# Top-128 rows of a gated scan through one expert: a last gather with a single wait, halved steps in the last expert block, another last search, one transfer for the weights

## Chip, cores and metric

One core of a Trainium2 chip runs the whole program. The metric is device time in microseconds (us). Times inside the program are counted from the start of the profiled span.

## The reference

Two steps, in float32. First a gated linear scan over 6208 positions, for 4 batches and 256 channels:

```python
f = lower_bound + (1 - lower_bound) * sigmoid(f_logit);  i = 1 - f
for t in range(S):                        # S = 6208
    h = f[:, t] * h + i[:, t] * x[:, t]
    y[:, t] = h
```

Then, for each batch, the 128 positions with the highest score go through one expert, and only these rows change:

```python
scores = einsum('bsd,d->bs', y, w_gate)
top = argpartition(-scores[b], 128)[:128]
xe = y[b, top]                            # 128 x 256
ye = maximum(xe @ w1, 0) @ w2             # w1 256 x 1024, w2 1024 x 256
out[b, top] = xe + sigmoid(scores[b, top])[:, None] * ye
```

## The kernel before

**Stream.** Channels lie on the 128 partitions in two halves (`h`), positions run along the free axis. The 6208 positions of a batch are cut into units of up to four blocks of 256. For each unit SP loads gate logits (`ft`) and inputs (`xt`), ACT makes the gates, POOL and DVE weigh the inputs, DVE runs the scan (L291), PE computes scores into the PSUM tile `score` (L300, one half of it for each batch in turn) and transposes the result into `pt`, ACT or DVE copies it to `ym`, and SP stores `ym` to the batch's output tensor (L327).

**Search** (`choose`, L372). For each batch: ACT copies the scores out (`keep`), PE spreads them over 32 lanes (`lanes`), DVE finds 16 candidates a lane and their places (`top`, `where`), PE broadcasts the candidates (`row`), DVE counts for four groups of candidates how many are greater (`ranks`), POOL and DVE make one-hot marks of the ranks (`marks`), PE pulls the indices out (`pull`), and DVE writes them to `idx` (`finish`, L458). A flag (`tell`, `flag`) says whether a lane had too many; its sum over the batches decides about the rare slow path below.

**Expert** (`stages`, L493, `experts`, L561). POOL gathers the 128 rows from the stored output by an indirect DMA (`fetch`, L502); it must wait for all stores of that batch and for `idx`. PE transposes the rows (`turn_in`, L508), ACT copies them out (`take`, L515), DVE computes the gate's score (`ask`, L524) and ACT its sigmoid (`opened`, L528). PE multiplies by w1 (`up`, L536: 8 groups x 2 halves, in float32 two records each), ACT applies relu to 4 groups at a time (L544), PE multiplies by w2 (`down`, L549: 8 groups), DVE adds the result to the rows (`mix`, L552) and POOL scatters them back (`scatter`, L556).

**Slow path** (`redo_all`, L636). DVE sums the flags into `total` (L638). POOL, PE, ACT and DVE each load `total` into a register (L639) and jump over the code of the slow path (L640), which is not run when the sum is zero. On POOL that code is some 7,000 instructions long. Each engine reads its instructions in order, so what stands behind the jump on an engine waits for the jump. The last batch's `mix` and `scatter` stand behind it.

**Order.** A planner (`Plan`, L58) simulates queues with a cost and a due time for each step and emits the steps in the order of their simulated start, so the order on each engine is fixed when the program is built. Waiting is by semaphores. On POOL an instruction with several waits is preceded by sequencer instructions (EVENT_SEMAPHORE) that carry two waits each.

Of the kernel before, what the change touches and what calls it, by code (L numbers as in the profile page):

```python
# [9 lines left out]
F32 = mybir.dt.float32  # L10
BF16 = mybir.dt.bfloat16
I32 = mybir.dt.int32
# [20 lines left out]
RUSH = [3]  # L33
XFER = 2.48
AHEAD, BACKLOG, STORE = 30.0, 4.0, 180.0
TURN, PUT, FIND, EXPERT = 20.0, 5.0, [0.0, -100.0, -50.0, -100.0], [240.0, -100.0, 80.0, 200.0]
WEIGHTS_AT = [6, 7]
AFTER = "pull"
HOP, PE_HOP, ISSUE, DONE = 0.14, 0.22, 1.75, 0.75
# [139 lines left out]
def gated_scan_moe(tc, xin, fin, lbwg, w1, w2, outs, cap):  # L179
    nc = tc.nc  # L180
    v, a, pe, g = nc.vector, nc.scalar, nc.tensor, nc.gpsimd
    with ExitStack() as ctx:
# [41 lines left out]
        w1t = const.tile([P, NH, F], F32, name="w1t")  # L224
        w2t = const.tile([P, NF, D], F32, name="w2t")
# [24 lines left out]
        def unit(i):  # L250
# [83 lines left out]
            plan.tile(("ym", i), (small, "y"), [("store", i)])  # L334
# [35 lines left out]
            add("sp", XFER * k, store, p + STORE, [*puts, ("store", i - 1)], ("store", i), late=DONE)  # L370

        def choose(b):  # L372
# [17 lines left out]

            def lanes():
                for k in range(BLK // LANE):
                    q0, c = (0, k - 6) if k >= 6 else (1, k + 2)
                    pe.matmul(acc[:LANE, c : c + 8 * (NBLK - q0) + 1 : 8], wide[b][:, k * LANE : (k + 1) * LANE],
                              order[:, q0 : NBLK + 1], start=True, stop=True)

            def top(k):
                if k == 0:
                    st["ci"] = new("ci", [LANE, 2, LEVELS])
                    st["at"] = new("at", [LANE, LEVELS], U32)  # L400
                    st["rest"] = new("rest", [LANE, NPOS])
                here, ci = acc[:LANE, :NPOS], st["ci"]
                if k == 0:
                    v.max(out=ci[:, 0, :TOP], in_=here)
                if k == 1:
                    v.max_index(out=st["at"][:, :TOP], in_max=ci[:, 0, :TOP], in_values=here)
                if k == 2:
                    v.match_replace(out=st["rest"], in_to_replace=ci[:, 0, :TOP], in_values=here, imm_value=LOW)
                if k == 3:
                    v.max(out=ci[:, 0, TOP:], in_=st["rest"])  # L410

            def spread():
                st["diag"] = d = new("dg", [LANE, RANKED, LANE])
                eye = acc[:LANE, A_ID : A_ID + LANE] if b in RUSH else ident[:LANE, :LANE]
                (v if b in RUSH else g).tensor_tensor(d, eye.unsqueeze(1).to_broadcast([LANE, RANKED, LANE]),
                                st["ci"][:, 0, :RANKED].unsqueeze(2).to_broadcast([LANE, RANKED, LANE]), ALU.mult)
# [4 lines left out]
            def number_of():  # L421
                (v if b in RUSH else g).tensor_copy(st["ci"][:, 1], st["at"])

# [3 lines left out]
            def own(what):  # L427
                for q in range(4):
                    pe.matmul(acc[q * LANE : (q + 1) * LANE, A_OWN + what * OWN : A_OWN + (what + 1) * OWN], ident[:LANE, :LANE],
                              st["ci"][:, what].rearrange("p (a q) -> p a q", q=4)[:, :, q], start=True, stop=True)  # L430

            def mine():
                st["mine"] = new("mine", [P, OWN])
                v.tensor_copy(st["mine"], acc[:, A_OWN : A_OWN + OWN])

            def ranks(k):
                if k == 0:
                    st["rank"] = new("rank", [P, OWN])
                junk = new("junk", [P, ROW], BF16)
                v.tensor_scalar(junk, acc[:, :ROW], st["mine"][:, k : k + 1], None, ALU.is_gt, ALU.add,  # L440
                                accum_out=st["rank"][:, k : k + 1])

            def number():
                v.tensor_scalar(vals[:, :, 0], acc[:, A_OWN + OWN : A_OWN + 2 * OWN], float(LANE), None, ALU.mult)

            def marks(k):
                if k == 0:
                    st["hot"] = new("hot", [P, OWN, P], BF16)
                (v if b in RUSH and k == OWN - 1 else g).tensor_scalar(st["hot"][:, k], slot, st["rank"][:, k : k + 1], None, ALU.is_equal)  # L449

# [20 lines left out]
            chain("pe", 0.8, lanes, extra=[("flag", b - 1), ("wgrow",), *[("mix", c) for c in range(b) if c not in APART]])  # L471
            for k in range(4):
                chain("dve", 0.4, lambda k=k: top(k))
            rush = b in RUSH
# [3 lines left out]
            m = chain("dve", 0.16, mine)  # L478
            w = chain("dve" if rush else "pool", 0.17, number_of, after=chain("dve", 0.44, where, after=t), extra=[d])
            r = chain("pe", 0.75, row, after=d)  # L480
            n = chain("dve", 0.17, number, after=chain("pe", 0.15, lambda: own(1), after=w, extra=[r]))
            marked = [n]
            for k in range(OWN):
                r = chain("dve", 0.74, lambda k=k: ranks(k), after=r, extra=[m])
                here = rush and k == OWN - 1
                marked.append(chain("dve" if here else "pool", 0.25 if here else 0.62, lambda k=k: marks(k), after=r))
            last[0] = r
# [5 lines left out]
        def stages(b, st):  # L493
            def fetch():
                again = "found" in st
                spot = st.get("spot")
                st["xe"] = spot[:, 3 * BLK : 4 * BLK] if again else rows[b % 2]
                st["res"] = spot[:, BLK : 2 * BLK] if again else moe.tile([P, D], F32, name="res", bufs=2)
                if again:
                    g.memset(st["xe"], 0.0)  # L500
                st["from"] = bass.IndirectOffsetOnAxis(ap=(st["found"] if again else chosen[b])[:cap, :], axis=0)
                g.indirect_dma_start(out=st["xe"][:cap, :], out_offset=None, in_=outs[b][:, :], in_offset=st["from"],  # L502
                                     bounds_check=S - 1, oob_is_err=False)

            def turn_in():
                st["px"] = st["bank"][1] if "found" in st else hold(("pm", b, 0), [P, TP * P], "pm")
                for h in range(NH):
                    pe.transpose(st["px"][:, h * P : (h + 1) * P], st["xe"][:, h * P : (h + 1) * P], ident)  # L508

# [16 lines left out]
            def opened():  # L526
                st["open"] = moe.tile([P, 1], F32, name="open" + "2" * ("found" in st), bufs=2)
                a.activation(st["open"], st["gate"], ACTF.Sigmoid)  # L528

# [20 lines left out]

            def mix():
                v.scalar_tensor_tensor(st["res"], st["py"][:, :D], st["open"], st["xe"], ALU.mult, ALU.add)  # L552
# [5 lines left out]

            return fetch, turn_in, take, ask, opened, up, relu, down, mix, scatter

        def experts(b):  # L561
            fetch, turn_in, take, ask, opened, up, relu, down, mix, scatter = stages(b, {})
# [4 lines left out]
            add("pool", 1.04, fetch, p0, [("st", b), ("store", last_unit[b])], k("fetch"))  # L567
            add("sw", 0.36, None, p0 - 1e3, [k("fetch")], k("xe"), late=LAND[b])
            add("pe", 0.36, turn_in, p0, [k("xe"), ("moe", b - 1, "down", NF - 1)], k("flip"), takes=[("pm", b, 0)])
            plan.tile(("pm", b, 0), ("pt", "pt"), [("xT", b)])  # L570
            add("act", 0.38, take, p0 - 1, [k("flip")], ("xT", b))
# [5 lines left out]
            for f in range(NF):  # L577
                add("pe", 0.49, lambda f=f: up(f), p0, [("xT", b), k("up", f - 1)], k("up", f), takes=[("pm", b, 1 + f // TP)] if f % TP == 0 else [])
# [3 lines left out]
            for f in range(NF):  # L582
# [71 lines left out]
        def weights(t, src, k):  # L654
            nc.sync.dma_start(t, src.rearrange("(p k d) -> p k d", p=P, k=k))
# [3 lines left out]
        for k, (t, src, n) in enumerate([(w1t, w1, NH), (w2t, w2, NF)]):  # L659
            add("sp", XFER, lambda t=t, src=src, n=n: weights(t, src, n), 20.0 * WEIGHTS_AT[k], [("x", WEIGHTS_AT[k])], ("w", k), late=DONE)  # L660
# [6 lines left out]
        plan.tile(("warm",), ("gt", "gt"), [("moe", B - 1, "down", 0)])  # L667
        add("pe", FILL, lambda: fill(True), 20.0 * N, [("forget", N - 1, 1)], ("warm",), takes=[("warm",)])
        plan.warm, plan.fill = (("warm",), ("moe", B - 1, "down", 0)), fill
# [45 lines left out]
```

## Time and profile before

| what | us |
|---|---|
| median of 3 runs (lowest, highest) | 212.48 (211.96, 212.50) |
| profiled execution, its own time | 211.78 |
| its span from first to last instruction | 209.8 |
| what lies around the span | 1.98 |

| engine | busy us | share of the span |
|---|---|---|
| PE (TensorE matmul) | 160.9 | 77% |
| DVE (VectorE) | 158.2 | 75% |
| ACT (ScalarE) | 154.1 | 73% |
| POOL (GpSimd) | 160.1 | 76% |
| DMA queue of SP (share of 16 engines' span) | | 89.6% |

How to read it: no engine is busy all the time, and the share of the SP queue's transfers is an average over a long stream in which the DMA engines are full and a tail of some 20 us in which they are nearly idle. The two have to be looked at apart. Rows with a name such as POOLq or PEldq are those of an engine's sequencer: waits, register loads, jumps.

### The profile page before, as it was taken

Reading aid. Unit: us, or ns where it says so; the run is one execution under the profiler, and the core shown is the slowest. Engines: PE = TensorE matmul, PEld = TensorE weight load, DVE = VectorE, ACT = ScalarE, POOL = GpSimd, SP = SyncE. Lnnn points to the kernel's source line nnn. Section 1 sums busy time; section 2 is a strip of 40 time slices with the busy share of each in tenths; the row PEclk is TensorE's granted clock in tenths of the full one; section 3 lists DMA queues with packets and bytes.
Section 4 is the critical chain, followed back from the end, with each engine's and each line's share of the span. In section 5 each row is a group of like instructions: output and inputs, shape, how many; then the busy total and the mean of one; then the engine's idle time right before and its main releaser. Section 6 shows DMA issues by size and latency. Waiting matters only on the chain. (4 is left out here: it accounts for less than half of the span.)

```text
span 209.8 us, 3352 instructions
## 1 busy us (share of the span) xinstructions
PE 160.9 (77%) x1174; PEld 104.5 (50%) x1174; DVE 158.2 (75%) x200; ACT 154.1 (73%) x206; POOL 160.1 (76%) x154
## 2 busy tenths in 40 slices
PE   0686749677878776773878998778789998989880
PEld 0233435444344444441435886444388856559670
DVE  1488599988799998868598969899795899472100
ACT  4698989989869899799769959768978787312110
POOL 4389999875989999987999895797999899223101
PEclk9997976999555899997559999995559999999996
DMA  6999999999999999999999999999999999992100
GB/s 203 407 428 426 426 425 419 429 428 420 414 433 426 422 422 427 426 428 425 419 428 428 418 420 430 423 417 425 430 426 425 419 422 417 430 417 82 52 5 28
DMA packets 13684, 79.69 MB, mean 380 GB/s; under 512 B 1760, under 2 KB 2016, under 8 KB 5728
## 3 DMA queue, kind: packets, MB, share of 16 engines
q1 hardware_dynamic: 13136, 78.39, 89.6%
q0 software_dynamic: 384, 1.05, 1.3%
q8 instruction: 11, 0.18, 0.3%
q14 instruction: 9, 0.07, 0.1%
q10 hardware_dynamic: 144, 0.00, 0.0%
HBM read 53.48 MB, written 25.95 MB: 379 GB/s over the span
## 5 line engine op out<-in xcount | busy, mean ns | idle before, releaser
L291 DVE TENSOR_TENSOR_SCAN xt<-gt,xt 128x1024 f32<-128x1024 f32 (+4 forms) x58 | 114.2, 1985 | 19.1 <-POOL xt L281 16.3
L281 POOL TENSOR_TENSOR xt<-xt,ft 128x1024 f32<-128x1024 f32 (+13 forms) x54 | 91.5, 1700 | 6.9 <-ACT ft L269 4.0
L307 PE MATMUL pt<-ident,xt 128*128 128x128 f32 x384 | 71.7, 331 | 5.1 <-ACT ym L324 3.2
L307 PEld LDWEIGHTS pt<-ident,xt 128*128 128x128 f32 x384 | 55.9, 204 | 32.1 <-ACT ym L324 14.6
L300 PE MATMUL score<-xt,wgr 128*32 128x256 f32 (+1 forms) x400 | 44.8, 463 | 29.9 <-DVE xt L291 29.2
L273 ACT ACTIVATE gt<-ft,nl 128x1024 f32<-128x1024 f32 (+4 forms) x58 | 56.9, 985 | 8.8 <-DVE xt L291 7.2
L277 POOL TENSOR_SCALAR xt<-xt,nl 128x1024 f32<-128x1024 f32 (+13 forms) x54 | 46.3, 861 | 13.7 <-DMA xt<-x 10.6
L269 ACT ACTIVATE ft<-ft 128x2048 f32<-128x2048 f32 (+4 forms) x29 | 47.3, 1632 | 10.0 <-DMA ft<-fl 10.0
L324 ACT COPY ym<-pt 128x512 f32<-128x512 f32 (+1 forms) x93 | 48.5, 555 | 7.9 <-PE pt L307 7.6
L300 PEld LDWEIGHTS score<-xt,wgr 128*32 128x32 f32 x400 | 9.9, 118 | 42.5 <-DVE xt L291 31.1
L536 PE MATMUL pm<-xT,w1t 128*128 128x128 f32 x128 | 17.5, 298 | 0.0
L536 PEld LDWEIGHTS pm<-xT,w1t 128*128 128x128 f32 x128 | 16.5, 210 | 1.4 <-ACT xT L515 1.0
L449 POOL TENSOR_SCALAR hot<-slot,rank 128x128 bf16<-128x128 bf16 x15 | 9.0, 607 | 9.1 <-DVE junk L440 8.6
L288 DVE SCALAR_TENSOR_TENSOR xt<-gt,xt 128x640 f32<-128x640 f32 (+10 forms) x22 | 14.1, 643 | 2.4 <-ACT gt L273 2.4
L556 POOL DMA_INDIRECT out<-res,aim x4 | 4.2, 1050 | 10.9 <-DVE res L552 10.4
L440 DVE TENSOR_SCALAR_CACHE_REDUCE junk<-acc,mine 128x448 bf16<-128x448 f32 x16 | 10.9, 682 | 0.7 <-PE acc L425 0.3
L549 PE MATMUL acc<-w2t,hT 128*128 128x256 f32 x48 | 11.0, 381 | 0.0
L544 ACT ACTIVATE hT<-pm 128x512 f32<-128x512 f32 x8 | 4.8, 595 | 7.9 <-PE pm L536 7.9
L549 PEld LDWEIGHTS acc<-w2t,hT 128*128 128x128 f32 x48 | 8.9, 190 | 1.5 <-issue 0.4
L515 ACT COPY xT<-pm 128x256 f32<-128x256 f32 x4 | 1.5, 373 | 9.4 <-PE pm L508 9.3
L552 DVE SCALAR_TENSOR_TENSOR res<-acc,open,xe 128x256 f32<-128x256 f32 x3 | 1.4, 481 | 8.9 <-PE acc L549 8.9
L502 POOL DMA_INDIRECT xe<-out,idx x4 | 4.6, 1148 | 4.4 <-DVE tally L468 3.3
(73 smaller groups left out, 78.2 us busy)
## 6 DMA issues: line engine op xcount, KB each, us to landing
ft<-fl SPq DMA_DIRECT2D x20, 1024.0 KB, 15.6
xt<-x SPq DMA_DIRECT2D x20, 1024.0 KB, 16.2
out<-ym SPq DMA_DIRECT2D x20, 1024.0 KB, 16.0
ft<-fl SPq DMA_DIRECT2D x3, 832.0 KB, 15.8
xt<-x SPq DMA_DIRECT2D x3, 832.0 KB, 15.7
out<-ym SPq DMA_DIRECT2D x3, 768.0 KB, 17.1
out<-ym SPq DMA_DIRECT2D x5, 256.0 KB, 14.5
ft<-fl SPq DMA_DIRECT2D x4, 256.0 KB, 15.5
```

What stands on the lines that cost most here:

```text
L269: a.activation(fs[i], fs[i], ACTF.Sigmoid, scale=-1.0)
L273: a.activation(gs[i, h][:, :n], fs[i][:, h], ACTF.Identity, scale=nl[:, h : h + 1], bias=1.0)
L277: g.tensor_scalar(xs[i][:, h, c0:], xs[i][:, h, c0:], nl[:, h : h + 1], 1.0, ALU.mult, ALU.mult)
L281: g.tensor_tensor(xs[i][:, h, c0:], xs[i][:, h, c0:], fs[i][:, h, c0:], ALU.mult)
L288: v.scalar_tensor_tensor(xs[i][:, h, :c1], gs[i, h][:, :c1], 1.0, xs[i][:, h, :c1], ALU.subtract, ALU.mult)
L291: v.tensor_tensor_scan(xs[i][:, h], gs[i, h][:, :n], xs[i][:, h], carry[h] if blk0 else 0.0, ALU.mult, ALU.subtract)
L300: pe.matmul(score[j * CG : (j + 1) * CG, b % 2, c0:], wgr[:, h, CG - 1 - r : 2 * CG - 1 - r], xs[i][:, h, c + c0 : c + BLK], start=(h == 0 ...
L307: pe.transpose(pts[key][:, q * P : (q + 1) * P], xs[i][:, h, tail + c :: cols], ident)
L324: (v.tensor_copy if eng == "dve" else a.copy)(out, src)
L440: v.tensor_scalar(junk, acc[:, :ROW], st["mine"][:, k : k + 1], None, ALU.is_gt, ALU.add, accum_out=st["rank"][:, k : k + 1])
L536: pe.matmul(st["pm", f // TP][:, c : c + P], w1t[:, h, f * P : (f + 1) * P], st["xT"][:, h], start=(h == 0), stop=(h == NH - 1))
L549: pe.matmul(st["py"][:, :D], st["hT"][:, f], w2t[:, f], start=(f == 0), stop=(f == NF - 1))
```

## The change

- The last batch's gather waits for the landing of one store only. The waits for `idx` and for the other stores of that batch are met ahead of it by small POOL instructions: a copy of one column (`copy_indices`) and, for each store, a write of one element of the stored tile (`see`).
- The last batch's expert: PE transposes the two halves into two tiles (`turn_half`), ACT copies one and DVE the other (`take_half`); `up` runs four groups with the first half, then with the second (`up_half`); `down` runs 128 columns of the output at a time (`down_half`), and so does the mix (`mix_half`). The second half of the mix is behind the slow path's jump, the first is not.
- The last batch's search uses the free half of `score` instead of `acc`, so its `lanes` need not wait for earlier users of `acc`; the first `MAX_INDEX` comes later; two of its four rank counts are sums of signs on ACT; two marks are made by DVE.
- w1 and w2 lie in one tensor and come by one transfer.

```diff
+            bank = score[:, 1 - b % 2] if rush else acc
...
+                if k in SIGNED[b]:
+                    junk = new("junks", [P, ROW], BF16)
+                    a.activation(junk, acc[:, :ROW], ACTF.Sign, scale=-1.0, bias=st["mine"][:, k : k + 1], accum_out=st["sign"][:, k : k + 1])
+                    return
...
+            def settle():
+                k = min(SIGNED[b])
+                v.tensor_scalar(st["rank"][:, k:], st["sign"][:, k:], -0.5, (ROW - 1) / 2, ALU.mult, ALU.add)
...
+            def see(i):
+                for t in [yms[i][:1, 0, :1]] + ([yts[i][:1, :1]] if units[i][3] else []):
+                    g.memset(t, 0.0)
+            def copy_indices():
+                g.tensor_copy(moe.tile([P, 1], I32, name="index"), chosen[b])
...
+            def take_half(h):
+                st["xT", h] = moe.tile([P, P], F32, name=f"xT{h}")
+                (v.tensor_copy if h else a.copy)(st["xT", h], st["px", h][:, :P])
...
+            def down_half(f, h):
+                if f == 0 and h == 0:
+                    st["py"] = acc
+                pe.matmul(st["py"][:, h * P : (h + 1) * P], st["hT"][:, f], w2t[:, f, h * P : (h + 1) * P], start=(f == 0), stop=(f == NF - 1))
...
+            if halved:
+                add("pool", 0.15, copy_indices, p0, [("st", b)], ("index", b))
+                for i in range(last_unit[b - 1] + 1, N - 1):
+                    add("pool", 0.1, lambda i=i: see(i), p0, [("store", i), ("index", b), ("seen", i - 1)], ("seen", i))
...
-            add("dve", 0.5, mix, p0 - 1, [("redo",) if b == B - 1 else k("down", NF - 1), ("scatter", b - 1), k("open")], ("mix", b))
+            if halved:
+                add("dve", 0.33, lambda: mix_half(0), p0 - 1, [k("downh", NF - 1), ("scatter", b - 1), k("open")], k("mixh"))
+                add("dve", 0.33, lambda: mix_half(1), p0 - 1, [("redo",), k("mixh"), k("open")], ("mix", b))
+            else:
+                add("dve", 0.5, mix, p0 - 1, [k("down", NF - 1), ("scatter", b - 1), k("open")], ("mix", b))
...
-        for k, (t, src, n) in enumerate([(w1t, w1, NH), (w2t, w2, NF)]):
-            add("sp", XFER, lambda t=t, src=src, n=n: weights(t, src, n), 20.0 * WEIGHTS_AT[k], [("x", WEIGHTS_AT[k])], ("w", k), late=DONE)
+        for k in range(2):
+            add("sp", XFER, weights if k == 1 else None, 20.0 * WEIGHTS_AT[k], [("x", WEIGHTS_AT[k])], ("w", k), late=DONE)
```

How the built order moves. Line numbers are those of each version. First DVE, from the flag of the last search to the last mix, before (`tally` are the flags, `res` the rows to be scattered, `py` and `acc` the expert's results):

```order
L467 SCALAR_TENSOR_TENSOR aim<-acc,idx 128x1 [waits DMASW3_49,PE_49]
L468 COPY tally<-acc 128x1
L552 SCALAR_TENSOR_TENSOR res<-py,open,xe_107 128x256 [waits PE_49,Activation_49]
L524 SCALAR_TENSOR_TENSOR res,gate<-xe_108,wgrow 128x256 [waits DMASW5_49]
L638 TENSOR_REDUCE total<-tally 1x1 [waits DVE_49]
L639 TENSOR_LOAD total [waits DVE_49]
L640 COMPARE_AND_BRANCH
...
L552 SCALAR_TENSOR_TENSOR res<-acc,open,xe_108 128x256 [waits PE_49,Activation_49]
```

And with the change:

```order
L480 COPY tally<-acc 128x1
L604 SCALAR_TENSOR_TENSOR res<-py,open,xe_107 128x256 [waits PE_49,Activation_49]
L559 SCALAR_TENSOR_TENSOR res,gate<-xe_108,wgrow 128x256 [waits DMASW5_49]
L543 COPY xT_1866<-pm 128x128 [waits PE_49]
L601 SCALAR_TENSOR_TENSOR res<-acc,open,xe_108 128x128 [waits PE_49,Activation_49]
L716 TENSOR_REDUCE total<-tally 1x1
L717 TENSOR_LOAD total [waits DVE_49]
L718 COMPARE_AND_BRANCH
...
L601 SCALAR_TENSOR_TENSOR res<-acc,open,xe_108 128x128 [waits PE_49]
```

The sum of the flags stood in front of every use of the last expert's products; now the first half of the mix, which waits for PE, stands in front of it. Then POOL, from the last marks to the jump, before:

```order
L449 TENSOR_SCALAR hot<-slot,rank 128x128 [waits DVE_49] x3
L502 DMA xe_108<-out,idx 128x256 [waits DMAHW4_49,DMAHW3_49,DMAHW5_49,DMAHW2_49,DMAHW6_49,DMAHW1_49,DMAHW7_49,DMAHW0_49,DVE_49]
L556 DMA out<-res,aim 6208x256 [waits DMASW4_49,DVE_49]
L639 TENSOR_LOAD total [waits DVE_49]
L640 COMPARE_AND_BRANCH
```

And with the change:

```order
L519 COPY index<-idx 128x1 [waits DVE_49]
L516 MEMSET ym 1x1 [waits DMAHW5_49]
L516 MEMSET yt 1x1 [waits DMAHW6_49]
L516 MEMSET ym 1x1 [waits DMAHW7_49]
...
L516 MEMSET ym 1x1 [waits DMAHW2_49,Activation_49]
L516 MEMSET ym 1x1 [waits DMAHW3_49,Activation_49]
L529 DMA xe_108<-out,idx 128x256 [waits DMAHW4_49]
L608 DMA out<-res,aim 6208x256 [waits DMASW4_49,DVE_49]
L717 TENSOR_LOAD total [waits DVE_49]
L718 COMPARE_AND_BRANCH
```

The gather's nine waits became one, with the others on a copy and seven one-element writes ahead of it (two like the third left out here); what stands behind the gather kept its order.

## Rows read from the trace of the kernel before

**Rows 1.** The page's slices: mean busy share of the 16 DMA engines, in tenths, in 40 equal slices of the span.

```profile
DMA  6999999999999999999999999999999999992100
```

**Rows 2.** Stretches of the tail: from:to, length, busy time (and count) of PE, PEld, DVE, ACT and POOL, granted TensorE clock, DMA share, GB/s.

```profile
186.00:188.00 2.00, 1.86 (x20) 1.49 (x20) 1.38 (x5) 0.20 (x1) 0.62 (x1) 1.00 1.03 434
...
190.00:191.00 1.00, 1.00 (x12) 0.96 (x11) 0.23 (x2) 0.39 (x1) 0.00 (x0) 1.00 0.20 76
...
192.00:194.50 2.50, 2.50 (x13) 1.91 (x11) 0.06 (x1) 0.00 (x0) 1.10 (x1) 1.00 0.00 0
```

**Rows 3.** The last store of the last batch (line L327, stretch 181.5 to 200): duration of the issue in ns (min/median/max), its start in us, and the time to its landing.

```profile
L327 SPq DMA_DIRECT2D out<-ym x1: 506/506/506, 182.0 to 182.0; - x1
...
DMA to landing us min/median/max: 9.8/9.8/9.8
```

**Rows 4.** The last gather (line L502, stretch 188.5 to 196): its sequencer waits, the gather itself (ns, first and last start in us), and its time to landing.

```profile
L502 POOLq EVENT_SEMAPHORE  x4: 43/43/43, 191.2 to 192.0; - x4
...
L502 POOL DMA_INDIRECT xe<-out,idx x1: 1104/1104/1104, 192.8 to 192.8; - x1
...
DMA to landing us min/median/max: 2.8/2.8/2.8
```

**Rows 5.** The timeline of the tail: start and length in us, engine, line, operation, tiles, shapes, count, and the idle time before with what ended it.

```profile
190.69 0.16 DVE L458 TENSOR_REDUCE idx<-acc 128x1 int32<-128x2 f32 x1 [0.86 <-PE acc L453]
...
192.80 1.10 POOL L502 DMA_INDIRECT xe<-out,idx  x1 [3.29 <-DVE tally L468]
...
194.44 0.48 DVE L552 SCALAR_TENSOR_TENSOR res<-py,open,xe 128x256 f32<-128x256 f32 x1 [2.52 <-PE py L549]
195.21 1.03 POOL L556 DMA_INDIRECT out<-res,aim  x1 [1.30 <-DVE res L552]
195.67 0.43 DVE L524 SCALAR_TENSOR_TENSOR res<-xe,wgrow 128x256 f32<-128x256 f32 x1 [0.74 <-DMA xe<-out,idx]
...
195.78 0.41 PE L508 MATMUL pm<-ident,xe 128*128 128x128 f32 x2 [1.02 <-DMA xe<-out,idx]
...
196.02 0.14 DVE L638 TENSOR_REDUCE total<-tally 1x1 int32<-1x4 f32 x1
...
196.28 0.37 ACT L515 COPY xT<-pm 128x256 f32<-128x256 f32 x1 [5.07 <-PE pm L508]
...
196.71 3.84 PE L536 MATMUL pm<-xT,w1t 128*128 128x128 f32 x32
...
200.38 3.62 PE L549 MATMUL acc<-w2t,hT 128*128 128x256 f32 x16
200.58 0.60 ACT L544 ACTIVATE hT<-pm 128x512 f32<-128x512 f32 x1 [1.13 <-PE pm L536]
204.12 0.48 DVE L552 SCALAR_TENSOR_TENSOR res<-acc,open,xe 128x256 f32<-128x256 f32 x1 [7.96 <-PE acc L549]
204.88 0.99 POOL L556 DMA_INDIRECT out<-res,aim  x1 [8.64 <-DVE res L552]
```

**Rows 6.** The jump over the slow path (line L640), sequencers of POOL, DVE, ACT and PE: ns, first and last start in us.

```profile
L640 POOLq EVENT_SEMAPHORE  x5: 17/42/43, 199.5 to 199.9; - x5
L640 POOLq COMPARE_BRANCH  x1: 53/53/53, 196.8 to 196.8; - x1
...
L640 DVEq EVENT_SEMAPHORE  x1: 21/21/21, 197.0 to 197.0; - x1
...
L640 ACTq COMPARE_BRANCH  x1: 45/45/45, 201.1 to 201.1; - x1
L640 ACTq EVENT_SEMAPHORE  x1: 17/17/17, 201.3 to 201.3; - x1
L640 PEldq COMPARE_BRANCH  x1: 3697/3697/3697, 201.8 to 201.8; - x1
```

**Rows 7.** The chain of work that ended last, in order of time (start, length, what): the last of POOL's waits ahead of the last scatter, and the piece behind it.

```profile
200.46 0.04 POOLq L556
200.50 4.15 issue
```

**Rows 8.** DMA in the stretch 197 to 200: busy share in 40 slices of 75 ns, and (packets, MB, share) the queue that loads POOL's code.

```profile
DMA  9710000000002000000000000000000000000000
...
q14 instruction: 1, 0.01, 0.6%
```

**Rows 9.** DMA in the stretch 206 to 207: busy share in 40 slices of 25 ns, and the queue that loads PE's code.

```profile
DMA  0000000090000000009489949948494440000000
...
q8 instruction: 1, 0.02, 7.0%
```

**Rows 10.** The scatter at 195.21 (line L556, stretch 190 to 200), time to landing.

```profile
DMA to landing us min/median/max: 2.5/2.5/2.5
```

**Rows 11.** The scatter at 204.88 (line L556, stretch 198 to 210), time to landing.

```profile
DMA to landing us min/median/max: 3.5/3.5/3.5
```

**Rows 12.** The timeline, other places: a one-column POOL memset, a copy of 512 columns on ACT, and the last search's place lookup and a rank count on DVE.

```profile
0.24 0.10 POOL L708 MEMSET const-float32-0.0<- 128x1 f32 x1 [0.24 <-issue]
...
179.34 0.59 ACT L324 COPY ym<-pt 128x512 f32<-128x512 f32 x1 [0.91 <-PE pt L307]
...
182.92 0.35 DVE L406 FIND_INDEX8 at<-ci,acc 32x8 uint32<-32x194 f32 x1
...
186.27 0.68 DVE L440 TENSOR_SCALAR_CACHE_REDUCE junk<-acc,mine 128x448 bf16<-128x448 f32 x1 [0.26 <-PE acc L425]
```

More of the change, by code (lines that the diff above doesn't have):

```diff
@@ L333, in unit @@
             plan.tile(("xt", i), (small, "x"), [("turn", i), ("scores", i, 1)])
-            plan.tile(("ym", i), (small, "y"), [("store", i)])
+            plan.tile(("ym", i), (small, "y"), [("store", i)] + [("seen", i)] * (b == B - 1 and i < N - 1))
             add("sp", XFER * k, lambda: load(fs, "ft", fin), p - AHEAD, [("f", i - 1)], ("f", i), late=DONE, takes=[("ft", i)])
@@ L369, in unit @@
             puts = [("putpart", e[1]) for e in ends] + ([("putpart", (i, "tail"))] if tail else [])
-            add("sp", XFER * k, store, p + STORE, [*puts, ("store", i - 1)], ("store", i), late=DONE)
+            add("sp", XFER * k, store, p + STORE + EXTRA[i], [*puts, ("store", i - 1)], ("store", i), late=STORED)
         def choose(b):
@@ L389, in keep @@
                 a.copy(wide[b], score[:, b % 2])
+            rush = b in RUSH
+            bank = score[:, 1 - b % 2] if rush else acc
+            own0 = NPOS + OWN if rush else A_OWN
             def lanes():
@@ L421, in number_of @@
             def number_of():
-                (v if b in RUSH else g).tensor_copy(st["ci"][:, 1], st["at"])
+                (v if rush else g).tensor_copy(st["ci"][:, 1], st["at"])
             def row():
@@ L448, in marks @@
                     st["hot"] = new("hot", [P, OWN, P], BF16)
-                (v if b in RUSH and k == OWN - 1 else g).tensor_scalar(st["hot"][:, k], slot, st["rank"][:, k : k + 1], None, ALU.is_equal)
+                (v if rush and k in (SIGNED[b] or [OWN - 1]) else g).tensor_scalar(st["hot"][:, k], slot, st["rank"][:, k : k + 1], None, ALU.is_equal)
             def pull():
@@ L470, in choose @@
             chain("act", 0.4, keep, ("keep", b), extra=[("scores", last_unit[b], 1)])
-            chain("pe", 0.8, lanes, extra=[("flag", b - 1), ("wgrow",), *[("mix", c) for c in range(b) if c not in APART]])
-            for k in range(4):
+            calm = [("flag", b - 1), ("wgrow",), *[("mix", c) for c in range(b) if c not in APART]]
+            chain("pe", 0.8, lanes, extra=[] if rush else calm)
+            for k in (0, 2, 3) if rush else range(4):
                 chain("dve", 0.4, lambda k=k: top(k))
-            rush = b in RUSH
             t = last[0]
@@ L478, in choose @@
             m = chain("dve", 0.16, mine)
+            if rush:
+                t = chain("dve", 0.44, lambda: top(1), after=t, extra=[d])
             w = chain("dve" if rush else "pool", 0.17, number_of, after=chain("dve", 0.44, where, after=t), extra=[d])
-            r = chain("pe", 0.75, row, after=d)
-            n = chain("dve", 0.17, number, after=chain("pe", 0.15, lambda: own(1), after=w, extra=[r]))
-            marked = [n]
+            r = chain("pe", 1.0 if rush else 0.75, row, after=d, extra=calm if rush else ())
+            marked = [chain("dve", 0.17, number, after=chain("pe", 0.15, lambda: own(1), after=w, extra=[r]))]
+            ranked, s = [], r
             for k in range(OWN):
+                if k in SIGNED[b]:
+                    s = chain("act", 0.74, lambda k=k: ranks(k), after=s, extra=[m])
+                    continue
                 r = chain("dve", 0.74, lambda k=k: ranks(k), after=r, extra=[m])
-                here = rush and k == OWN - 1
+                here = rush and not SIGNED[b] and k == OWN - 1
                 marked.append(chain("dve" if here else "pool", 0.25 if here else 0.62, lambda k=k: marks(k), after=r))
+            if SIGNED[b]:
+                r = chain("dve", 0.16, settle, after=s, extra=[r])
+                marked += [chain("dve", 0.25, lambda k=k: marks(k), after=r) for k in SIGNED[b]]
             last[0] = r
@@ L508, in turn_in, with turn_half @@
                     pe.transpose(st["px"][:, h * P : (h + 1) * P], st["xe"][:, h * P : (h + 1) * P], ident)
+            def turn_half(h):
+                st["px", h] = hold(("pm", b, -h), [P, TP * P], "pm")
+                pe.transpose(st["px", h][:, :P], st["xe"][:, h * P : (h + 1) * P], ident)
+            def take_half(h):
+                st["xT", h] = moe.tile([P, P], F32, name=f"xT{h}")
+                (v.tensor_copy if h else a.copy)(st["xT", h], st["px", h][:, :P])
             def take():
@@ L528, in opened, with up_half @@
                 a.activation(st["open"], st["gate"], ACTF.Sigmoid)
+            def up_half(f0, h):
+                if h == 0:
+                    st["pm", f0 // TP] = hold(("pm", b, 1 + f0 // TP), [P, TP * P], "pm")
+                for f in range(f0, f0 + TP):
+                    c = f % TP * P
+                    pe.matmul(st["pm", f0 // TP][:, c : c + P], w1t[:, h, f * P : (f + 1) * P], st["xT", h], start=(h == 0 and f == f0),
+                              stop=(h == NH - 1), skip_group_check=True)
             def up(f):
@@ L557, in scatter @@
                                      bounds_check=S - 1, oob_is_err=False)
+            st["half"] = turn_half, take_half, up_half, down_half, mix_half, copy_indices, see
             return fetch, turn_in, take, ask, opened, up, relu, down, mix, scatter
         def experts(b):
-            fetch, turn_in, take, ask, opened, up, relu, down, mix, scatter = stages(b, {})
+            st = {}
+            fetch, turn_in, take, ask, opened, up, relu, down, mix, scatter = stages(b, st)
+            turn_half, take_half, up_half, down_half, mix_half, copy_indices, see = st["half"]
+            halved = b == B - 1
             p0 = 20.0 * last_unit[b] + EXPERT[b]
@@ L566, in experts @@
             prev = ("mix", b - 1)
-            add("pool", 1.04, fetch, p0, [("st", b), ("store", last_unit[b])], k("fetch"))
+            if halved:
+                add("pool", 0.15, copy_indices, p0, [("st", b)], ("index", b))
+                for i in range(last_unit[b - 1] + 1, N - 1):
+                    add("pool", 0.1, lambda i=i: see(i), p0, [("store", i), ("index", b), ("seen", i - 1)], ("seen", i))
+            add("pool", 1.04, fetch, p0, [("st", b), ("index", b), ("seen", N - 2) if halved else None, ("store", last_unit[b])], k("fetch"))
             add("sw", 0.36, None, p0 - 1e3, [k("fetch")], k("xe"), late=LAND[b])
-            add("pe", 0.36, turn_in, p0, [k("xe"), ("moe", b - 1, "down", NF - 1)], k("flip"), takes=[("pm", b, 0)])
             plan.tile(("pm", b, 0), ("pt", "pt"), [("xT", b)])
-            add("act", 0.38, take, p0 - 1, [k("flip")], ("xT", b))
+            if halved:
+                plan.tile(("pm", b, -1), ("pt", "pt"), [("xT", b, 1)])
+                for h in range(NH):
+                    add("pe", 0.18, lambda h=h: turn_half(h), p0 - 2, [k("xe"), ("moe", b - 1, "down", NF - 1), k("flip", h - 1)], k("flip", h), takes=[("pm", b, -h)])
+                    add("dve" if h else "act", 0.28, lambda h=h: take_half(h), p0 - 2, [k("flip", h)], ("xT", b, h) if h else ("xT", b))
+            else:
+                add("pe", 0.36, turn_in, p0, [k("xe"), ("moe", b - 1, "down", NF - 1)], k("flip"), takes=[("pm", b, 0)])
+                add("act", 0.38, take, p0 - 1, [k("flip")], ("xT", b))
             if b in ASKED:
@@ L576, in experts @@
             add("act", 0.22, opened, p0 - 1, [k("ask")], k("open"))
-            for f in range(NF):
+            for f0 in range(0, NF, TP) if halved else ():
+                for h in range(NH):
+                    add("pe", 0.95, lambda f0=f0, h=h: up_half(f0, h), p0, [("xT", b, h) if h else ("xT", b), k("up", f0 - 1), k("uph", f0) if h else None],
+                        k("up", f0 + TP - 1) if h else k("uph", f0), takes=[("pm", b, 1 + f0 // TP)])
+            for f in range(0 if halved else NF):
                 add("pe", 0.49, lambda f=f: up(f), p0, [("xT", b), k("up", f - 1)], k("up", f), takes=[("pm", b, 1 + f // TP)] if f % TP == 0 else [])
@@ L581, in experts @@
                 add("act", 0.6, lambda f0=f0: relu(f0), p0 - 1, [k("up", f0 + TP - 1)], k("relu", f0))
-            for f in range(NF):
+            for h in range(NH if halved else 0):
+                for f in range(NF):
+                    add("pe", 0.24, lambda f=f, h=h: down_half(f, h), p0, [k("relu", f // TP * TP), k("up", NF - 1), k("downh", NF - 1) if h else None, k("down" if h else "downh", f - 1), k("ask"), ("flag", b)],
+                        k("down" if h else "downh", f), load=1.0)
+            for f in range(0 if halved else NF):
                 add("pe", 0.46, lambda f=f: down(f), p0, [k("relu", f // TP * TP), k("up", NF - 1), k("down", f - 1), k("ask"), None if b in APART else ("flag", b),
```

45 lines of the change are left out of this document (25 added, 20 removed).

## Prediction

> **What bounds the kernel now.** I read the page's slices first: the DMA engines are full for nine tenths of the span and nearly idle after it [rows 1]. The stretches of the tail say where that flips: 434 GB/s at 186 to 188, 76 at 190 to 191, nothing at 192 to 194.5, with the TensorE clock granted in full throughout [rows 2]. So there are two kernels to judge. Up to the last store the program moves its bytes, and an edit that leaves the bytes alone gains nothing there. Behind it comes a single file of dependent steps, in which every step is the bound while it runs, and there the change is made.
>
> The timeline gives the single file [rows 5]. The last store is issued at 182.0 and lands 9.8 later, at 191.8 [rows 3]; the indices were ready at 190.69 + 0.16 = 190.85, a microsecond before, so the store releases the gather. The gather starts at 192.80 and lands 2.8 later, at 195.6 [rows 4]. Then transpose 195.78, copy 196.28, `up` 196.71, `down` 200.38, mix 204.12, scatter 204.88, whose data land 3.5 later, at 208.4 [rows 5, 11]. The last 1.4 us of the span are the closing handshake.
>
> One part is hidden: the jump over the slow path. DVE sums the flags at 196.02, as soon as it has scored the gathered rows [rows 5]. POOL loads the sum at 196.2 and jumps at 196.8, but its next instruction is at 199.5, and its last wait ahead of the scatter ends at 200.46 + 0.04 = 200.50 [rows 6, 7]. From the end of the sum (196.16) that is 4.34 us. It costs nothing now, because the mix ends only at 204.60: POOL is ready with 4.1 us to spare, the piece of 4.15 in the chain [rows 7].
>
> **The change, part by part.** I follow the start of the last scatter, 204.88 before.
>
> *Weights, search, small POOL work: 0.* One transfer of 2 MB replaces two of 1 MB in the full stretch; the bytes are the same. I bound it by the spread of the runs shown, 0.5 us, either way. The search loses a lookup of 0.35 + its load and two of four rank counts of 0.68 on DVE, gains two sums on ACT (0.59 for a copy of 512 columns is the nearest row) [rows 12] and a second DVE mark; it ends earlier, but it is covered by the last store (191.8 against 190.85), and would cost only if it grew by a microsecond. The POOL copy and seven memsets (0.10 each [rows 12]) wait for stores that land before the last one and are covered by it. Nothing but the gather is queued behind them on POOL.
>
> *The gather's waits: -0.70.* Before, the gather starts 0.98 after the last landing, behind four sequencer waits that run from 191.2 to 192.05 [rows 4]. With the wait in the instruction itself the nearest rows are the two scatters, which start 0.28 after the mix they wait for (194.92 to 195.21, 204.60 to 204.88 [rows 5]). So it starts at 192.10. The other end: only what the waits take after the landing goes, 192.05 - 191.8 = some 0.2. I take 0.70, since gather and scatter are the same kind of instruction.
>
> *Transposes in halves: -0.25.* From the first transpose to `up` took 0.93. One of two transposes saves some 0.16 of 0.41; a copy of 128 columns instead of 256 saves 0.11 of 0.37 by the slope from 256 columns (0.37) to 512 (0.59) [rows 5, 12]; ends 0.1 and 0.3. DVE's copy of the second half stands behind the scoring, which ends about 0.3 after the first transpose, and even at the whole 0.37 is ready 0.1 or so after ACT's; PE wants it after eight records of the first half, 0.9 after `up` starts. Covered. `up` keeps its 32 records and 3.84 us.
>
> *`down` in halves: +0.10.* 32 records of 128 columns take 3.84 where 16 of 256 took 3.62 [rows 5], but only the first half matters below. The second relu (200.58 to 201.18) was needed four groups into `down`, 1.7 after its start; now 0.9 after it, which is 0.8 + a handover: 0.1 of waiting (0 to 0.1). So `down` effectively starts at 200.38 - 0.70 - 0.25 + 0.10 = 199.53 and its first half ends 2.0 later (half of 3.84 and the overhang of a record), at 201.53.
>
> *The sum of the flags: the cover is gone.* In the new order DVE has the first half of the mix ahead of the sum. The mix starts 0.12 after PE's end, as before (204.00 to 204.12 [rows 5]), and takes about 0.32 (0.48 for 256 columns, 0.16 for one): 201.97. The sum overlaps it by 0.07 and ends at 202.04, where it ended at 196.16 before. Queued behind it are DVE's own jump, over 1.0 after the sum's start (196.02 to 197.0 [rows 5, 6]) and so in time for the second half of `down` (199.53 + 3.84 = 203.4), and POOL's, which is not: 202.04 + 4.34 = 206.38. The second half of the mix is done at 203.4 + 0.12 + 0.32 = 203.8; POOL makes it wait 2.5 us. After its last wait POOL still has to take up the scatter; the gather of before, which also stood directly behind sequencer waits, started 0.75 after the last of them (192.05 to 192.80 [rows 4]). If that work were already done, it would be 0.28. I take 0.75: 207.13, which is 2.25 later than before.
>
> *The landing: -1.0.* The scatter at 195.21 landed after 2.5, the last one after 3.5 [rows 10, 11]. In the latter's time a load of PE's code begins at 206.2, and the scatter's packets start at 206.45 and trail on it [rows 9]. PE's jump started at 201.8, took 3.70, and the load came 0.7 after it and was 1.1 long (7.0% of sixteen engines for 1 us) [rows 6, 9]. With the sum at 202.04, and 0.64 from the sum to a jump as on POOL, PE's jump starts at 202.7 and that load lies at 207.1 to 208.2; the packets (1.57 after the scatter's start) begin at 208.7. So I take 2.5; the other end is 3.5.
>
> Sum: +2.25 - 1.0 = +1.25 us. On the profiled execution's own 211.78 that is 213.0; that execution lies 0.7 below the median of the runs, so by the median it is 212.48 + 1.25 = **213.7**.
>
> **Rivals.** A measurement of this kernel tells about 0.3% (0.64 us) from no change, so "same" is 211.84 to 213.12.
>
> *A, faster: POOL's jump is short when nothing else is under way.* ACT's jump was over 0.2 after it began [rows 6]. POOL's would then be ready at 202.04 + 0.64 + 0.2 + 1.0 (199.5 to 200.50) = 203.9, the scatter starts at 204.6 and lands 2.5 to 3.5 later, 0.3 to 1.3 earlier than before: about 211.7. The point from which it decides: the gap from sum to last wait would have to be under 3.1 us instead of 4.34 for no loss. Against it: POOL's jump took 2.7 and PE's 3.7, and both engines load code right behind it [rows 6, 8, 9]; ACT and DVE skip a few dozen instructions, POOL some 7,000. I give 0.12. [...]
>
> *B, same: the jump is shorter by a part.* When POOL jumped at 196.8, the packets of the scatter before were under way, and the code load came about 1.1 later, at 197.9 [rows 6, 8]. In the new place no scatter is in flight. If half to all of that 1.1 goes, +0.15 to +0.7 is left: 212.9. Against it: PE's jump had idle DMA engines and took longer. 0.13. [...]
>
> *C, slower still: the gather gains only 0.2, or the last scatter meets PE's code load again.* +0.5 or +1.0: 214.2 to 214.7. 0.15. The margin of the second is 0.5 us (208.2 against 208.7).
>
> **How the numbers follow.** The forecast has 0.60, with a range of its own of 213.2 (taking up in 0.28) to 214.2. Only A is faster: 0.13 with the odd case. Same: B and its neighbours, 0.14. Slower: 0.73. The range 212.3 to 214.9 takes in B and most of C with the 0.5 us either way of the full stretch, and leaves out A and the far end of C.
>
> **What would show it.** Gather within 0.35 of the last landing; `up` about 0.95 earlier than before; the sum of the flags directly behind the first half of the mix, near 202; POOL's jump over only near 206, with the second half of the mix long done; the last scatter near 207 and landing after 2.5. The forecast is wrong if POOL's waits end before the second half of the mix, or if the last store lands elsewhere than near 191.8, since then the full stretch has moved, which I hold for unmoved.

## The result: 0.8% slower, near the forecast

The changed kernel takes 213.87 us (median of 6 runs, 213.22 to 214.32) against 212.22 (6 runs, 211.70 to 212.63) beside it: ratio 1.0083, 95% interval 1.0062 to 1.0104. The forecast was 213.7, slower. The profiled execution took 213.8, its span 211.9. All medians here are over all runs; the ratios leave out one run of 214.05, of the kernel with short code below, which lies over 1.5% above the fastest run of that kernel.

The timeline of the changed kernel's tail, the columns as in [rows 5]:

```profile
191.41 0.09 POOL L516 MEMSET ym<- 1x1 f32 x1 [0.93 <-DMA out<-ym]
192.22 1.10 POOL L529 DMA_INDIRECT xe<-out,idx  x1 [0.72 <-DMA out<-ym]
...
195.28 0.41 PE L539 MATMUL pm<-ident,xe 128*128 128x128 f32 x2 [0.43 <-DMA xe<-out,idx]
...
195.62 0.27 ACT L543 COPY xT<-pm 128x128 f32<-128x128 f32 x1 [4.13 <-PE pm L539]
...
195.96 3.82 PE L570 MATMUL pm<-xT,wt 128*128 128x128 f32 x32
...
199.61 2.23 PE L597 MATMUL acc<-wt,hT 128*128 128x128 f32 x18
...
201.96 0.35 DVE L601 SCALAR_TENSOR_TENSOR res<-acc,open,xe 128x128 f32<-128x128 f32 x1 [5.94 <-PE acc L597]
202.23 0.13 DVE L716 TENSOR_REDUCE total<-tally 1x1 int32<-1x4 f32 x1
...
202.37 1.83 PE L597 MATMUL acc<-wt,hT 128*128 128x128 f32 x14 [0.52 <-DVE total L716]
204.24 0.35 DVE L601 SCALAR_TENSOR_TENSOR res<-acc,open,xe 128x128 f32<-128x128 f32 x1 [1.87 <-PE acc L597]
207.65 0.99 POOL L608 DMA_INDIRECT out<-res,aim  x1 [11.15 <-issue]
```

The front of the tail is faster: `up` starts at 195.96 instead of 196.71. The end is slower: the mix is done at 204.59, as early as before, but the scatter starts at 207.65, 3.06 after the end of the mix instead of 0.28. Its idle time ends in "issue", that is, by nothing an engine or a DMA released. What stood there is POOL's sequencer; the jump in the changed kernel, as [rows 6]:

```profile
L718 POOLq EVENT_SEMAPHORE  x5: 17/43/43, 205.9 to 206.2; - x5
...
L718 POOLq COMPARE_BRANCH  x1: 53/53/53, 203.0 to 203.0; - x1
```

and the end of its chain, as [rows 7]:

```profile
206.83 0.04 POOLq L608
206.88 0.55 issue
```

Before, POOL's last wait was followed by a piece of 4.15 us in which POOL stood ready; now by one of 0.55. The scatter starts 0.23 after the end of that piece in both, so taking it up costs 0.77 from the last wait. The last store, as [rows 3], landed at 181.8 + 10.1 = 191.9, a tenth later than before:

```profile
L329 SPq DMA_DIRECT2D out<-ym x1: 596/596/596, 181.8 to 181.8; - x1
...
DMA to landing us min/median/max: 10.1/10.1/10.1
```

The landing of the last scatter took 2.4. The stretch 207 to 210 (slices of 75 ns) shows the load of PE's code well ahead of the scatter's packets, where the packets trailed on the load before [rows 9, 11]. The profile names the queue of such a load and not the engine; q8 is taken for PE's, since a load on it starts 0.6 to 1.0 us after the end of PE's jump record in the four kernels read for it (before, changed, e1, e8). The load is one packet and shows in the slice in which it starts, 207.15; the share of its queue, 2.5% of 16 engines over 3 us, makes it 1.2 us long. So it ends near 208.4, and the scatter's packets start near 209.2:

```profile
DMA  0090000000000000000000000000099997100000
...
q8 instruction: 1, 0.02, 2.5%
```

### The profile page after: what moved, and what is told of

It is laid out like the page before. It is cut to its first block, busy times and chain, and to the rows that moved or that the text cites. A ratio compares the mean times of both kernels' runs of the same rounds, so it can differ in the third digit from the quotient of the medians.

```text
span 211.9 us, 3390 instructions
## 1 busy us (share of the span) xinstructions
PE 155.7 (73%) x1188; PEld 101.2 (48%) x1188; DVE 157.6 (74%) x200; ACT 155.3 (73%) x210; POOL 159.8 (75%) x161
## 5 line engine op out<-in xcount | busy, mean ns | idle before, releaser
L309 PE MATMUL pt<-ident,xt 128*128 128x128 f32 x384 | 68.9, 320 | 5.4 <-ACT ym L326 4.1
L309 PEld LDWEIGHTS pt<-ident,xt 128*128 128x128 f32 x384 | 54.1, 202 | 31.6 <-ACT ym L326 15.1
L302 PE MATMUL score<-xt,wgr 128*32 128x256 f32 (+1 forms) x400 | 43.5, 449 | 32.8 <-DVE xt L293 31.8
L275 ACT ACTIVATE gt<-ft,nl 128x1024 f32<-128x1024 f32 (+4 forms) x58 | 56.9, 985 | 10.1 <-DVE xt L293 6.5
L579 PE MATMUL pm<-xT,wt 128*128 128x128 f32 x96 | 12.2, 281 | 0.0
L579 PEld LDWEIGHTS pm<-xT,wt 128*128 128x128 f32 x96 | 11.2, 192 | 1.1 <-ACT xT L550 0.7
L448 DVE TENSOR_SCALAR_CACHE_REDUCE junk<-acc,mine 128x448 bf16<-128x448 f32 x14 | 9.6, 682 | 2.3 <-ACT junks L445 2.0
L326 DVE COPY ym<-pt 128x512 f32<-128x512 f32 (+1 forms) x11 | 6.9, 625 | 1.4 <-PE pt L309 1.4
L592 PE MATMUL acc<-wt,hT 128*128 128x256 f32 x32 | 7.3, 382 | 0.0
L592 PEld LDWEIGHTS acc<-wt,hT 128*128 128x128 f32 x32 | 5.9, 190 | 1.1 <-issue 0.4
L431 PE MATMUL acc<-dg,onesf 32*128 32x448 f32 x8 | 4.7, 673 | 2.1 <-POOL dg L421 2.1
```

What stands on the lines that cost most here:

```text
L275: a.activation(gs[i, h][:, :n], fs[i][:, h], ACTF.Identity, scale=nl[:, h : h + 1], bias=1.0)
L302: pe.matmul(score[j * CG : (j + 1) * CG, b % 2, c0:], wgr[:, h, CG - 1 - r : 2 * CG - 1 - r], xs[i][:, h, c + c0 : c + BLK], start=(h == 0 ...
L309: pe.transpose(pts[key][:, q * P : (q + 1) * P], xs[i][:, h, tail + c :: cols], ident)
L326: (v.tensor_copy if eng == "dve" else a.copy)(out, src)
L579: pe.matmul(st["pm", f // TP][:, c : c + P], w1t[:, h, f * P : (f + 1) * P], st["xT"][:, h], start=(h == 0), stop=(h == NH - 1))
L592: pe.matmul(st["py"][:, :D], st["hT"][:, f], w2t[:, f], start=(f == 0), stop=(f == NF - 1))
```

## The experiments

Theory U: POOL's jump has come into the open, because the sum of the flags stands behind the first half of the mix. Rival P: PE, with more records in the halved product and a wait for DVE. Rival S: the full stretch, the search or the weights. Each kernel has a label, and its first two characters stand for it. The kernels e1, e5, e6 and e8 ran beside one set of runs of the kernel before (median 212.09), e2, e3, e4 and e9 beside another (212.16).

**The sum early (e1_sum_early).**

```diff
             chain("dve", 0.4, flag, ("flag", b))
+            if b == B - 1:
+                chain("dve", 0.2, add_up, ("sum",))     # the tensor_reduce taken out of redo_all
```

> The changed kernel with one edit: DVE sums the flags right behind the last flag, not behind the first half of the mix. Nothing else moves. Theory U (the loss is POOL's jump, uncovered because the sum stands behind the first half of the mix): POOL's waits end by 200.5, before the mix; the last scatter starts 0.28 after the second half of the mix, near 204.9, and lands 2.5 to 3.5 later: 211.1 to 212.1, that is 1.8 to 2.8 under the changed kernel. Rival P (the loss is on PE: more records in the halved product and PE's wait for DVE): nothing of that is undone, so the time stays at 213.9. Rival S (the full stretch or the search moved): stays at 213.9.

Measured 210.86, ratio 0.9952 (0.9935 to 0.9969). POOL's jump, and the timeline of the end:

```profile
L722 POOLq EVENT_SEMAPHORE  x5: 17/43/43, 198.4 to 198.7; - x5
L722 POOLq COMPARE_BRANCH  x1: 53/53/53, 195.5 to 195.5; - x1
```

```profile
202.21 1.83 PE L603 MATMUL acc<-wt,hT 128*128 128x128 f32 x14 [0.52 <-DVE res L607]
204.08 0.35 DVE L607 SCALAR_TENSOR_TENSOR res<-acc,open,xe 128x128 f32<-128x128 f32 x1 [1.92 <-PE acc L603]
204.71 0.99 POOL L614 DMA_INDIRECT out<-res,aim  x1 [8.37 <-DVE res L607]
```

The jump takes as long as ever (195.5 to 198.4) and is hidden again; the scatter is released by the mix, 0.28 after it. One instruction's place is worth 3.0 us between the two medians, more than the whole loss; the time lies 0.24 below the range that was expected for Theory U. As causes of the loss P and S fall: nothing of theirs was undone. PE's wait for DVE is still there, 0.52 in the first row. In the changed kernel the same wait is put down to the sum, `total`, which ends at about the same moment; here, where the sum is long done, it is the first half of the mix, `res`.

**The halves of the second product and the mix alone, on the kernel before (e3_mix_halves_alone).** `down_half`, `mix_half` and their `add` calls, as in the diff of the change, and nothing else of it.

> The kernel before with one part of the change: second product and mix of the last batch in halves, and with it the sum of the flags behind the first half of the mix. Theory U: this part alone makes the whole loss and more: the sum ends near 203.1, POOL's last wait 4.4 later, the scatter starts near 208.3 and lands after 2.5: 214.2 to 214.8. Rival P (the loss is only PE's extra records and its wait for DVE, 0.7): 212.9.

Measured 214.43, ratio 1.0106 (1.0083 to 1.0129). The timeline:

```profile
203.12 0.13 DVE L659 TENSOR_REDUCE total<-tally 1x1 int32<-1x4 f32 x1
...
205.13 0.35 DVE L558 SCALAR_TENSOR_TENSOR res<-acc,open,xe 128x128 f32<-128x128 f32 x1 [1.87 <-PE acc L554]
208.41 0.99 POOL L565 DMA_INDIRECT out<-res,aim  x1 [11.29 <-issue]
```

The sum ends at 203.25 and the scatter starts at 208.41, within 0.15 of what Theory U had; P's 212.9 is out. This part alone makes the loss. In the profiles the rest of the change gives 0.76 back (the scatter starts at 207.65 in the changed kernel); in time the intervals of the two ratios overlap.

**Short code to jump over (e8_short_code).** In `redo`, `for k in range(cap)` becomes `for k in range(1)`; the slow path, not run, is thereby incomplete.

> The changed kernel with one round instead of 128 in each of the slow path's four search loops (the slow path, which does not run here, would then choose wrongly): POOL's code to be jumped is about 100 instructions instead of some 7,200. The order of everything that runs is that of the changed kernel, the sum as late. Theory U with the code load as its price: the 2.9 us from POOL's jump to its next instruction shrink to about 0.2, POOL's waits end near 204.2, and the scatter starts near 205: 211.2 to 212.2. If the price is the handshake with the DMA queues or anything else that does not depend on the length of the code: 213.9.

Measured 211.25, ratio 0.9962 (0.9937 to 0.9987). POOL's jump, and the end of the timeline:

```profile
L718 POOLq EVENT_SEMAPHORE  x5: 17/43/43, 204.1 to 204.4; - x5
L718 POOLq COMPARE_BRANCH  x1: 45/45/45, 203.6 to 203.6; - x1
```

```profile
204.85 0.35 DVE L601 SCALAR_TENSOR_TENSOR res<-acc,open,xe 128x128 f32<-128x128 f32 x1 [1.87 <-PE acc L597]
205.82 0.99 POOL L608 DMA_INDIRECT out<-res,aim  x1 [9.15 <-DVE res L601]
```

Same late place, but 0.5 us instead of 2.9 from the jump to the next instruction. So the price hangs on the length of the code jumped over, at the two lengths tried, and is not the row of semaphore events behind the jump; that remains, about 1 us (204.1 to 205.06; 199.5 to 200.50 before). The scatter starts 0.8 later than expected. 0.6 of that is the profiled execution's last store, which landed at 192.59 instead of 191.94. For the rest, POOL's last wait ended at 205.06, just ahead of the mix (205.20), and POOL still took 0.76 from it to the scatter.

The loads of POOL's code fit this. DMA in the stretch 203 to 206 (slices of 75 ns), first of the changed kernel, then of this one; the last mark of each row is the load of POOL's code (q14):

```profile
DMA  0000000000009000200000000000000000000000
...
q14 instruction: 1, 0.01, 0.6%
```

```profile
DMA  0000000000000000000007200000000000000000
...
q14 instruction: 1, 0.01, 0.7%
```

In the changed kernel the load, near 204.2, lies between POOL's jump (203.0) and its next instruction (205.9), as it did before [rows 6, 8]; with the short code it comes near 204.7, when POOL is already past its next instruction (204.1). That q14 loads POOL's code is read from these times alone: its load starts 1.1 to 1.2 us after the start of POOL's jump in all three kernels. Why POOL goes on only 1.3 us after the end of a load that is 0.3 long is not shown.

**Whole mix (e5_whole_mix).** `down` and `mix` as before the change, the rest as changed.

> The changed kernel with the second product and the mix whole again, as before; gather, halved transposes, search and weights stay. The sum is then early by itself. Theory U: the second product starts at 199.6 and takes 3.62, the mix starts 0.12 later and takes 0.48, the scatter starts 0.28 after it, at 204.1: 210.4 to 211.4, faster than both kernels. Rival P: the same sign, but then e1_sum_early shows no gain. Rival S: stays at 213.9.

Measured 211.18, ratio 0.9956 (0.9936 to 0.9977). The scatter starts at 203.88, the earliest of all, but lands late. Its landing, and DMA in the stretch 205 to 206 (slices of 25 ns):

```profile
DMA to landing us min/median/max: 3.6/3.6/3.6
```

```profile
DMA  0000000000900000049499909949880800000000
...
q8 instruction: 1, 0.02, 7.2%
```

PE's code load, near 205.25, is again just ahead of the scatter's packets, which start near 205.43. What the scatter gains against e1 (0.83 us) the landing gives back (3.6 against 2.4).

**Two banks (e6_two_banks).** On e1, the second half of the product goes to the free half of `score`: `py = score[:, b % 2, :P] if h else st["py"][:, :P]`, in `down_half` and `mix_half`.

> e1_sum_early with the second half of the second product in another PSUM tile, so that PE need not wait for DVE's reading of the first half. Theory U with that wait as a second, now covered cost of 0.5 us: it shows once the jump is early, so this kernel is 0.5 under e1_sum_early and level with e5_whole_mix to 0.2 (scatter near 204.2, 210.5 to 211.5). If PE's wait has another cause than the shared tile: level with e1_sum_early. Rivals P and S: 213.4 and 213.9.

Measured 210.41, ratio 0.996 (0.993 to 0.999). The timeline:

```profile
199.67 2.01 PE L604 MATMUL acc<-wt,hT 128*128 128x128 f32 x16
...
201.52 1.95 PE L604 MATMUL score<-wt,hT 128*128 128x128 f32 x16
201.80 0.35 DVE L609 SCALAR_TENSOR_TENSOR res<-acc,open,xe 128x128 f32<-128x128 f32 x1 [5.72 <-PE acc L604]
203.50 0.35 DVE L609 SCALAR_TENSOR_TENSOR res<-score,open,xe 128x128 f32<-128x128 f32 x1 [1.36 <-PE score L604]
204.14 0.99 POOL L616 DMA_INDIRECT out<-res,aim  x1 [8.38 <-DVE res L609]
```

PE runs through and the scatter starts 0.57 before e1's, though the profiled execution's last store landed 0.22 later. So the tile shared by PE's second half and DVE's reading of the first was the cause of the 0.52. Counted from the start of `down`, the scatter starts after 4.47 instead of 5.25; 0.22 of the rest of this gain is the first half of the mix, which waits for 16 records instead of 18. The medians differ by 0.45, but the runs of this kernel spread more (209.9 to 212.9, against 210.8 to 211.3 of e1), and the intervals overlap: the gain is shown in the trace and not in the time. Level with e5, as expected, it is not: its median is 0.77 lower, and e5's landing, with PE's code load just ahead of its packets, was 1.2 longer.

**The gather alone, on the kernel before (e2_gather_alone).** `copy_indices`, `see` and their `add` calls.

> The kernel before with one part of the change: the last gather carries one wait, the others are met by the copy and the memsets (three fill matmuls that the planner would add in front of the last transposes are left out, as in the kernel before). The sum stays early. Theory U, part gather: it starts 0.28 after the last landing instead of 0.98, so the scatter moves 0.7 forward; if the code load of PE still delays the landing: 211.4, if not: 210.4. Rival G (only the waits behind the landing go): 211.9.

Measured 211.70, ratio 0.9976 (0.9955 to 0.9998), between the forecasts of U and G. The trace decides:

```profile
192.33 1.10 POOL L509 DMA_INDIRECT xe<-out,idx  x1 [0.73 <-DMA out<-ym]
...
204.45 0.99 POOL L563 DMA_INDIRECT out<-res,aim  x1 [8.45 <-DVE res L559]
```

The last store landed at 192.06, and the gather starts 0.27 after it, as in U, not G. The scatter is 0.43 earlier than before and not 0.70, since that store landed 0.24 later in this execution. The landing took 3.2 (3.5 before, and 2.5 in the better case of U), and the closing is 0.34 longer.

**Old search and old weight transfers, the rest as changed (e4_old_search).**

> The changed kernel with the old last search and the two old weight transfers (three fill matmuls left out as in e2_gather_alone); gather and halves as changed. Theory U: search and weights are covered, so level with the changed kernel, 213.4 to 214.2. Rival S: clearly below it, 212.2 to 213.

Measured 214.27, ratio 1.0113 (1.0078 to 1.0148): not below the changed kernel, which speaks against S. But its profile shows the cover of the search gone, which could hide a gain:

```profile
192.04 0.16 DVE L470 TENSOR_REDUCE idx<-acc 128x1 int32<-128x2 f32 x1 [0.87 <-PE acc L465]
...
192.27 0.18 POOL L517 COPY index<-idx 128x1 int32<-128x1 int32 x1 [1.41 <-DVE bad L472]
...
193.20 1.10 POOL L527 DMA_INDIRECT xe<-out,idx  x1 [0.54 <-issue]
```

The last store landed at 191.85; here the indices, at 192.20, came after it, and the gather starts 0.98 later than in the changed kernel. So this kernel alone does not rule S out. What does are e3, with the old search and weights and the whole loss, and e1, with the new ones and no loss. Whether the new search is worth anything in time stays open: the intervals of the two ratios overlap.

**Code moved (e9_page_moved).** On e6, `for _ in range(118): g.memset(rows[0][:1, :1], 0.0)` inside the slow path, which is jumped over: nothing more runs.

> [...] In the changed kernel, in e1, e5 and e6 POOL's closing instructions show one gap of 0.4 us that the kernel before and e8_short_code do not have. [...] Rival (it comes with the changed order of the tail): level with e6_two_banks, 210.4.

Measured 210.39, ratio 0.9938 (0.9900 to 0.9975). POOL's closing, of e6 and then of this kernel:

```profile
L795 POOLq EVENT_SEMAPHORE  x4: 17/17/17, 207.2 to 208.3; - x4
...
L795 POOLq EVENT_SEMAPHORE_RANGE_CLEAR  x1: 161/161/161, 207.5 to 207.5; - x1
```

```profile
L797 POOLq EVENT_SEMAPHORE  x4: 17/17/17, 207.4 to 208.0; - x4
...
L797 POOLq EVENT_SEMAPHORE_RANGE_CLEAR  x1: 161/161/161, 207.7 to 207.7; - x1
```

From the clear to the last instruction it is 0.36 instead of 0.70 (the rows round to a tenth): in these two profiles the gap goes when only code that never runs is added ahead of it. What makes the gap is not shown. The time came out as the rival had it: the medians of e6 and e9 do not show the gain (the last store of e9's profile landed 0.2 later). Both are below both kernels of the case.

## Why the prediction was right

- *The gather, -0.70:* 192.22 is 0.27 after the last landing, as taken (0.28); e2 shows the same by itself.
- *Transposes in halves, -0.25:* from the first transpose to `up` 0.68 instead of 0.93. As forecast.
- *First half of `down`:* under-sized by 0.13. The sum has 2.0 + 0.1 from the start of `down` to its end; it was 2.23, and the mix started 0.12 after that. PE had 18 records in front of the mix, not 16: DVE's wait counts the first group of the second half too. In e6, with the banks apart, 16 records take 2.01, and the mix again starts 0.12 after them.
- *PE's wait for DVE, 0.52:* missed; the prediction lets the second half follow the first without a pause. The second half of the mix was done at 204.59 instead of 203.8. It cost nothing, since POOL was later by 3 us; e6 against e1 shows its price without that cover.
- *The sum, the jump, the scatter:* the sum ended at 202.36 (202.04 forecast), POOL's last wait 4.52 later (4.34), the scatter 0.77 after that (0.75). This is the step that makes the sign; e1, e3 and e8 show it from three sides.
- *The landing, -1.0:* 2.4 instead of 3.5. In the kernel before and in e5 the scatter's packets start 0.2 to 0.3 behind the start of PE's code load (206.45 and 206.20; 205.43 and 205.25) and while it runs, 1.1 to 1.2 long, and land after 3.5 and 3.6. In e2 the landing took 3.2, and the place of that load is not shown. In the seven other kernels the first packets go out ahead of that load or behind its end, and they land after 2.4 to 2.6. That the load is the cause is read from these nine profiles; no run moves the load alone.
- *Not in the sum:* the closing grew by 0.34, the size of the gap that is gone in e9.

Between the two profiles these terms add up to 2.77 (the scatter, +2.25 forecast) - 1.06 (the landing) + 0.34 (the closing) = +2.05. Between the medians it is +1.65, where +1.25 was forecast. That 213.7 came so near to 213.87 is in part luck: it was reckoned from 212.48, the median of three runs, and six runs gave 212.22, from which the same sum makes 213.5.

Rival A falls with the changed kernel's 2.9 us from jump to next instruction, at a time when the DMA engines carried nothing but two loads of code. So does B, by which it should have become shorter than the 2.7 of before. The record of the jump itself lasted 53 ns on POOL in the kernel before, the changed kernel and e1 and 45 ns in e8, and on PE 3.3 to 3.9 us in the same four. C did not come: the margin to PE's code load was 0.8 instead of the 0.5 taken, since the scatter came later.

## What to carry to other kernels

A small check that sits in front of a jump should be issued as soon as its inputs exist, and not where its engine happens to be free: here DVE and POOL ran their instructions in the order in which the program was built, so half of the mix ahead of the check moved the check to the end of what that half waits for (from 196.0 to 202.2), and the scatter behind the jump started at 207.65, with the mix done at 204.59. Before a step is split, ask of every instruction that stood behind the whole step, on each engine, whether it now stands behind a half. The lowest medians came from keeping the split, with the sum early and the halves in two PSUM tiles (e6 and e9, 210.4). But the intervals of e1, e5 and e6 overlap, so no run here shows that splitting the second product beats leaving it whole.

## What the runs showed of the hardware

- A jump over some 7,000 POOL instructions took 2.7 to 2.9 us from its end to the next instruction (before, changed, e1), over about 100 instructions 0.44 us (e8), with the jump itself 45 to 53 ns.
- Indirect scatters whose packets started 0.2 to 0.3 us behind the start of a load of PE's code, and while it ran, took 3.5 and 3.6 us to landing (before, e5), those whose packets went out ahead of it or behind its end 2.4 to 2.6 (seven kernels). In e2, where the load's place is not shown, it was 3.2.
- An indirect DMA on POOL started 0.27 to 0.28 us after the event that it waited for when its wait was its own (gathers of the changed kernel and e2, scatters of before and e1), but 0.74 to 0.77 us after the last of separate sequencer waits right in front of it (the gather of before, the scatters of the changed kernel, e3 and e8).
- Adding code that never runs moved a 0.34 us gap out of POOL's closing sequence (e9 against e6, one profile each).
